# Fewer zero stores inside the groups of an attention-and-FFN backward kernel, the others issued after all compute, and the first weight load issued by ACT

## The chip, the cores and the metric

The kernel runs on one core of one Trainium2 chip. The metric is the device time in microseconds (us) of one execution. A time is the median of several executions. Every comparison was made in rounds on one chip (each of the three sets of experiments on a chip of its own), and runs marked slow (over 1.5% above the fastest of the same kernel) are left out of the ratios.

## The reference

A decode step of a parallel block is differentiated. In short form, the forward pass and what is returned are

```python
xn  = layernorm(x)                                       # x: 4 x 1 x 512, bf16
out = x + attention(xn; k_cache, v_cache, wq, wo) + (gelu(xn @ w_gate) * (xn @ w_up)) @ w_down
# attention: 32 query heads, 8 KV heads, Dh = 128; caches of 4096 positions, of which
# only the last W = 1024 are used:  k = k_cache[:, :, Sk - W:, :]
_out, _vjp = jax.vjp(f, x, k_cache, v_cache, wq, wo, w_gate, w_up, w_down)
return (_out, *_vjp(grad_out))
```

The outputs are `out` and eight gradients. Those of the two caches (`out_2`, `out_3`: 4 x 8 x 4096 x 128) are exactly zero in their first 3072 positions, since the window never reads them. Writing these zeros is 50.3 MB of the 112.4 MB that the kernel moves. They depend on nothing, so the kernel may write them at any time.

## The kernel before

The engines are named as in the profile. In this kernel PE does matmuls and transposes, DVE, ACT and POOL the elementwise work and copies, and SP, ACT and POOL issue transfers (DMA). The tiles that PE writes lie in PSUM here (names in `_ps`); copying a result out of one is called an evacuation. "Granted clock" is the profile's figure for the share of PE's full clock that it was given.

The kernel works through a feed-forward part and then four groups of two KV heads each. (Code below is cut to the lines that matter; `...` marks what is left out.) A zero store is one transfer of 3.146 MB from a tile of zeros, issued by ACT. There are sixteen (`zlist`). A small edge of order ties each to the last evacuation that ACT has been given so far.

```python
    ZG = 4
    zlist = [(og, b, g) for b in range(B) for g in range(0, G, ZG) for og in (out_2, out_3)]

    def zeros(n):
        zsrc = bass.AP(tensor=ztile.tensor, offset=ztile.offset, ap=[list(ztile[:].ap[0]), [0, ZG], [1, ZW]])
        for _ in range(min(n, len(zlist))):
            og, b, g = zlist.pop(0)
            z = store(nc.scalar, og[b, g:g + ZG, 0:K0, :].rearrange("g (m j) d -> m g (j d)", m=P), zsrc, "zeros",
                      ["rest", "zeros"])
            if last_act:
                tc.add_manual_dep(z.ins, last_act[-1].ins.name, ...NoSync...)
```

In the two score passes of a group, each block of K (then of V) is transposed on PE, copied from PSUM by DVE, and multiplied. A queue of small pieces of other work (`tick`) fills in. Each pass issues two zero stores:

```python
    def scores(t, k):
        # ... lf = masked queries (k = 0) or output gradients (k = 1)
        for g in range(GP):
            for b in range(B):
                T_ps = ps_w.tile([P, J, P], BF16, name="T_ps", tag="w")
                for j in range(J):
                    nc.tensor.transpose(T_ps[:, j, :], blks[(t, g)][:, b, j, :], ident[:])
                T_sb = tsb.tile([P, J * P], BF16, name="T_sb", tag="T", bufs=4)
                evac(T_sb[:], T_ps[:].rearrange("p j m -> p (j m)"), 1024, half=True)
                for q in range(NQ):
                    nc.tensor.matmul(ps[q * RG:(q + 1) * RG, :], lhsT=..., rhs=T_sb[...], ...)
                tick(2)
                if b == 1:
                    zeros(1)
```

The feed-forward part issues one more (`zeros(1 if og is out_6 else 0)`). All loads are on SP, in program order. The compiler's scheduler decides the order of the other engines' instructions; only SP is kept in program order.

```python
        nc.sync.dma_start(out=wg_sb[:], in_=B_w_gate...)     # then wu_sb, wd_sb, and the first groups' data
        # ...
        for t in range(NT):
            pre(t); masks(t)
            scores(t, 0); softmax(t);   dvdk(t, 0)
            scores(t, 1); softmax_d(t); dvdk(t, 1)
            odq(t, 0); odq(t, 1)        # od matmuls: values with P, keys with dS
            fin(t); load_next(t); dw(t)
        tick(len(bg))
        # ... two small outputs, issued by ACT
```

## Time and profile before

| | kernel before |
|---|---|
| median | 301.78 us (4 runs, 297.4 to 303.23; the two above 303 count as slow) |
| span of the profiled run | 297.0 us |
| busy shares | PE 71%, DVE 49%, ACT 38%, POOL 22% |
| moved | 112.38 MB, 378 GB/s over the span |
| mean granted clock of PE | 0.838 |

The strip of the page cuts the span into 40 slices; a digit is the busy share of a slice in tenths. The strip, the waits and the group starts stand in the prediction below. The short reading is that the transfers are full almost everywhere (the DMA row is 9 in 35 of 40 slices) and PE is not (71% busy).

### The profile page before, as it was taken

What the parts mean: (1) busy time and instruction counts of PE and PEld (TensorE: products, weight loads), DVE (VectorE), ACT (ScalarE), POOL (GpSimd) and SP (SyncE); (2) the same over time, 40 slices, a digit from 0 to 9 for tenths busy, and PEclk for the clock granted to TensorE, in tenths of its full rate; (3) what the DMA queues carried; (4) which work ended last, traced back from release to release, by engine and by line L of the source; (5) the groups of instructions that cost most, each with busy time, mean ns of one, the idle gap of its engine ahead of it and who ended that gap; (6) DMA issues with size and microseconds to landing.
All of it is one profiled execution on the core that took longest, in us unless ns stands there. A gap on an engine that the chain in (4) does not pass through costs nothing.

```text
span 297.0 us, 6830 instructions
## 1 busy us (share of the span) xinstructions
PE 209.5 (71%) x2956; PEld 144.7 (49%) x2956; DVE 144.7 (49%) x309; ACT 114.0 (38%) x217; POOL 66.4 (22%) x84
## 2 busy tenths in 40 slices
PE   1249897963977997587799066986941976869941
PEld 0249575741645774364576033754731544546321
DVE  6236574433553575345367023453640553544956
ACT  3010464543440665334166023442440453524850
POOL 6000112340303143310314302303010523130230
PEclk9999999695796899779699757697795697986995
DMA  5999999999999999999999999999999799993693
GB/s 150 401 350 386 395 418 397 408 419 424 421 415 414 384 370 419 416 420 418 418 418 421 416 421 420 419 414 418 417 413 404 280 389 391 389 400 146 239 340 131
DMA packets 34149, 112.38 MB, mean 378 GB/s; under 512 B 1408, under 2 KB 7560, under 8 KB 34120
## 3 DMA queue, kind: packets, MB, share of 16 engines
q10 hardware_dynamic: 8464, 50.34, 41.3%
q1 hardware_dynamic: 17848, 30.93, 28.3%
q0 software_dynamic: 7808, 30.67, 26.2%
q8 instruction: 23, 0.38, 0.5%
q14 instruction: 6, 0.05, 0.0%
HBM read 30.93 MB, written 81.01 MB: 377 GB/s over the span
## 4 chain that ended last, share of the span: by engine, by line
DMA 43%; PE 36%; DVE 11%; ACT 3%; issue 3%; POOL 1%; SPq 1%; DVEq 0%; ACTq 0%; POOLq 0%
DMA kb<-in_A_k_cache_dram 26%; PE T_ps L316 8%; DMA out_dram<-osb_o 6%; DMA wd_sb<-in_B_w_down_dram 6%; DVE T_sb L94 5%; PE kv_ps L424 5%; PE S_ps L321 3%; DMA out_dram<-osb_d 3%; DMA out_dram<-osb_g 3%; PE od_ps L396 2%; PE wdT_ps L561 2%; PE wqT_ps L488 2%; PE dwo_ps L443 2%; PE acc_ps L168 1%; PE dwg_ps L607 1%
## 5 line engine op out<-in xcount | busy, mean ns | idle before, releaser
L94 DVE COPY T_sb<-T_ps 128x1024 bf16<-128x1024 bf16 x64 | 44.2, 691 | 47.5 <-PE T_ps L316 47.3
L92 ACT CAST stg_dv<-kv_ps 128x512 bf16<-128x512 f32 x52 | 28.4, 588 | 30.7 <-PE kv_ps L424 30.4
L316 PE MATMUL T_ps<-ident,kb 128*128 128x128 bf16 x256 | 26.1, 245 | 19.0 <-DMA kb<-in_A_k_cache_dram 19.0
L316 PEld LDWEIGHTS <-kb 128*128 128x128 bf16 x256 | 19.9, 111 | 28.5 <-DMA kb<-in_A_k_cache_dram 19.6
L92 ACT CAST stg_dk<-kv_ps 128x512 bf16<-128x512 f32 x46 | 25.2, 588 | 12.8 <-PE kv_ps L424 12.1
L316 PE MATMUL T_ps<-ident,vb 128*128 128x128 bf16 x256 | 25.7, 247 | 0.3 <-DVE osb_q L94 0.3
L424 PE MATMUL kv_ps<-domr,P_q 128*128 128x512 bf16 x64 | 23.5, 441 | 0.0
L316 PEld LDWEIGHTS <-vb 128*128 128x128 bf16 x256 | 19.6, 112 | 6.0 <-issue 1.8
L92 ACT CAST osb_o<-dwo_ps 128x512 bf16<-128x512 f32 x23 | 12.9, 588 | 21.5 <-PE dwo_ps L443 21.0
L92 ACT CAST osb_g<-dwg_ps 128x384 bf16<-128x384 f32 (+1 forms) x30 | 14.7, 532 | 16.6 <-PE dwg_ps L607 8.7
L424 PE MATMUL kv_ps<-qmr,dS_q 128*128 128x512 bf16 x64 | 20.7, 394 | 0.5 <-ACT stg_dv L92 0.2
L92 ACT CAST osb_q<-dwq_ps 128x512 bf16<-128x512 f32 x25 | 13.7, 588 | 16.9 <-PE dwq_ps L458 10.4
L98 POOL DMA_DIRECT2D out_dram<-stg_dv x8 | 6.2, 776 | 40.3 <-ACT stg_dv L92 25.3
L94 DVE COPY wqT<-wqT_ps 128x1024 bf16<-128x1024 bf16 x16 | 11.0, 690 | 8.2 <-PE wqT_ps L488 8.1
L321 PE MATMUL S_ps<-T_sb,qm 128*32 128x256 bf16 x128 | 9.9, 302 | 6.9 <-DVE T_sb L94 6.8
L94 DVE COPY woT<-woT_ps 128x1024 bf16<-128x1024 bf16 x16 | 11.1, 692 | 6.3 <-PE woT_ps L268 6.3
L488 PEld LDWEIGHTS <-wq_sb 128*128 128x128 bf16 x128 | 11.4, 124 | 5.5 <-issue 4.9
L458 PE MATMUL dwq_ps<-od_r,xnm 128*128 128x256 bf16 x64 | 12.9, 328 | 1.2 <-DVE osb_q L94 1.0
L92 ACT CAST osb_d<-dwd_ps 128x512 bf16<-128x512 f32 x14 | 8.0, 590 | 14.5 <-PE dwd_ps L595 14.3
L321 PE MATMUL S_ps<-T_sb,dom 128*32 128x256 bf16 x128 | 10.0, 298 | 5.0 <-DVE T_sb L94 5.0
L321 PEld LDWEIGHTS <-qm 128*32 128x32 bf16 x128 | 4.7, 94 | 17.6 <-issue 15.8
L488 PE MATMUL wqT_ps<-ident,wq_sb 128*128 128x128 bf16 x128 | 13.3, 267 | 0.0
(186 smaller groups left out, 376.8 us busy)
## 6 DMA issues: line engine op xcount, KB each, us to landing
out_dram<-ztile ACTq DMA_DIRECT2D x16, 3072.0 KB, 18.5
kb<-in_A_k_cache_dram SPq DMA_DIRECT2D x8, 1024.0 KB, 12.1
vb<-in_A_v_cache_dram SPq DMA_DIRECT2D x8, 1024.0 KB, 24.6
out_dram<-stg_dv POOLq DMA_DIRECT2D x8, 1024.0 KB, 10.5
out_dram<-stg_dk POOLq DMA_DIRECT2D x8, 1024.0 KB, 11.0
wo_sb<-in_A_wo_dram SPq DMA_DIRECT2D x4, 1024.0 KB, 26.7
wq_sb<-in_A_wq_dram SPq DMA_DIRECT2D x4, 1024.0 KB, 30.5
out_dram<-osb_o POOLq DMA_DIRECT2D x8, 512.0 KB, 9.5
```

Of the source, the lines that this page charges most:

```text
L92: last_act.append(nc.scalar.copy(out=out, in_=in_))
L94: return nc.vector.tensor_copy(out=out, in_=in_)
L98: d = eng.dma_start(out=out, in_=in_)
L168: nc.tensor.matmul(ps[:, c, :], lhsT=lf(c), rhs=rhs, start=(k == 0), stop=(k == len(terms) - 1))
L316: nc.tensor.transpose(T_ps[:, j, :], blks[(t, g)][:, b, j, :], ident[:])
L321: nc.tensor.matmul(ps[q * RG:(q + 1) * RG, :], lhsT=lf[:, s * RG:(s + 1) * RG], rhs=T_sb[:, q * WQ:(q + 1) * WQ], start=(g == 0 and b == 0 ...
L396: nc.tensor.matmul(od_ps[b * RB:b * RB + rep, k, g, :], lhsT=pT[:, jj, c0:c0 + rep], rhs=blks[(t, g)][:, b, j, :], start=(j == 0), stop=(j ...
L424: nc.tensor.matmul(mps[:].rearrange("p b d -> p (b d)"), lhsT=src[:, q, jj * P:(jj + 1) * P], rhs=mr[:, g].rearrange("p b d -> p (b d)"), ...
L443: nc.tensor.matmul(mps[:], lhsT=o_r[:, g, :], rhs=dym[:, i, :], start=True, stop=True)
L458: nc.tensor.matmul(mps[:, i].rearrange("p g d -> p (g d)"), lhsT=xnm[:, i2 * 2 + i, c * P:(c + 1) * P], rhs=dq_r[:].rearrange("p g d -> p ...
L488: nc.tensor.transpose(wT_ps[:, i, c, :], wq_sb[:, c, h * Dh:(h + 1) * Dh], ident[:])
L561: nc.tensor.transpose(wT_ps[:, i, c, :], wd_sb[:, 2 * f2 + i, c * P:(c + 1) * P], ident[:])
```

## The change

The intent is to free the compute from the competition of the zero stores: one in each group, the others when nothing else is left to be disturbed. The load of the first weight moves to ACT, so that it starts beside SP's two small loads. The two small outputs move to SP, away from the long queue on ACT.

```diff
-                if b == 1:
+                if b == 1 and g == 1 and k == 0:
                     zeros(1)
@@
-        nc.sync.dma_start(out=wg_sb[:], in_=B_w_gate.rearrange("(c p) f -> p c f", p=P))
+        nc.scalar.dma_start(out=wg_sb[:], in_=B_w_gate.rearrange("(c p) f -> p c f", p=P))
@@
         tick(len(bg))
+        zeros(len(zlist))
@@
-        nc.scalar.dma_start(out=out_0..., in_=out_b[0:P:RB, :])
+        nc.sync.dma_start(out=out_0..., in_=out_b[0:P:RB, :])
@@
-        nc.scalar.dma_start(out=out_1..., in_=dx_b[0:P:RB, :])
+        nc.sync.dma_start(out=out_1..., in_=dx_b[0:P:RB, :])
```

More of the change, by code (lines that the diff above doesn't have):

```diff
@@ L676 @@
         nc.vector.tensor_tensor(out=out_b[:], in0=acc_o, in1=x_b[:], op=ALU.add)
-        nc.scalar.dma_start(out=out_0.rearrange("b s d -> (b s) d"), in_=out_b[0:P:RB, :])
+        nc.sync.dma_start(out=out_0.rearrange("b s d -> (b s) d"), in_=out_b[0:P:RB, :])
         s1 = tail.tile([P, 1], FP32, name="s1")
@@ L694 @@
         nc.vector.tensor_tensor(out=dx_b[:], in0=pr[:], in1=dy_b[:], op=ALU.add)
-        nc.scalar.dma_start(out=out_1.rearrange("b s d -> (b s) d"), in_=dx_b[0:P:RB, :])
+        nc.sync.dma_start(out=out_1.rearrange("b s d -> (b s) d"), in_=dx_b[0:P:RB, :])
 _INS = ['A_x', 'A_k_cache', 'A_v_cache', 'A_wq', 'A_wo', 'B_x', 'B_w_gate', 'B_w_up', 'B_w_down', 'grad_out']
```

## The prediction

Passages are cut out, with the cuts marked. The sum stands: 259 + 82 + 5 + 2 = 348 us of span, plus 1.7, about 350, put down as 349. The 82 us follow from the trace: 34.6 MB take 82.8 us at the 418 GB/s of many full slices and 81.6 at the 424 of the best one. The 2 us for the last landing are an estimate that fits the kernel before, where the issue of the last store ended at 294.98 us and the span at 297.0. That fewer stalls would make matmuls faster was the estimate from the one stretch quoted, where PE's clock was 0.56 after 9 us without work.

> **What bounds the kernel now.** I read the page first: the strip of 40 slices (7.4 us each), then the queues.
>
> ```profile
> PE   1249897963977997587799066986941976869941
> PEclk9999999695796899779699757697795697986995
> DMA  5999999999999999999999999999999799993693
> GB/s 150 401 350 386 395 418 397 408 419 424 421 415 414 384 370 419 416 420 418 418 418 421 416 421 420 419 414 418 417 413 404 280 389 391 389 400 146 239 340 131
> ...
> q10 hardware_dynamic: 8464, 50.34, 41.3%
> q1 hardware_dynamic: 17848, 30.93, 28.3%
> q0 software_dynamic: 7808, 30.67, 26.2%
> ```
>
> The reader is to see that the DMA row is 9 nearly everywhere while PE has holes. The transfers are the bound from slice 2 to slice 31, at 415 to 421 GB/s in most slices. The queue lines say what moves. q10, on which ACT issues, carries only the zero stores (16 of 3,072 KB = 3.146 MB each, 50.34 MB) and two tiny outputs. q1 has the loads (30.93 MB), q0 the computed gradients (30.67 MB). The three shares sum to 95.8%, some 285 us of full DMA work in a span of 297.0 us, so the kernel stands within about 12 us of its own transfers. Most of that loss is at the two ends (slices 1, 32, 37 to 40).
>
> Next the waits of PE, longest first, which say what the transfers cost the compute:
>
> ```profile
> PE T_ps L316 <- DMA kb<-in_A_k_cache_dram: 19.0, 2, 10.1
> PE S_ps L321 <- DVE T_sb L94: 11.8, 26, 0.8
> ...
> PE f_ps L672 <- ACT osb_q L92: 3.7, 1, 3.7
> ...
> PE dwg_ps L607 <- DVE osb_g L94: 3.5, 1, 3.5
> ...
> PE dwg_ps L607 <- ACT osb_g L92: 1.8, 1, 1.8
> ```
>
> Only 19.0 us of PE idleness is put down to late K blocks (8.9 and 10.1 us). Another 3.5, 1.8 and 3.7 us are evacuations that waited for an output buffer still being stored: ACT and DVE show waits for the stores of osb_g and osb_o in their own wait lists. That is 28 us in all that contention with the zero stores could have caused. The rest of PE's waits are short handoffs that stay. The chain of waits names the two K transfers:
>
> ```profile
> 144.15 28.48 DMA kb<-in_A_k_cache_dram
> ...
> 181.67 47.35 DMA kb<-in_A_k_cache_dram
> ```
>
> A 1,024 KB load takes 28 and 47 us to land because zero stores and gradients are ahead of or between it.
>
> Last the pace of the four groups, from the timeline of POOL, where dS_q is made once per group:
>
> ```profile
> 90.75 1.89 POOL L332 TENSOR_TENSOR dS_q<-dS_b,qmsk 128x1024 bf16<-128x1024 bf16 x1 [8.43 <-DVE dS_b L385]
> ...
> 142.20 1.88 POOL L332 TENSOR_TENSOR dS_q<-dS_b,qmsk 128x1024 bf16<-128x1024 bf16 x1 [8.36 <-DVE dS_b L385]
> ...
> 203.81 1.88 POOL L332 TENSOR_TENSOR dS_q<-dS_b,qmsk 128x1024 bf16<-128x1024 bf16 x1 [7.67 <-DVE dS_b L385]
> ...
> 265.22 1.89 POOL L332 TENSOR_TENSOR dS_q<-dS_b,qmsk 128x1024 bf16<-128x1024 bf16 x1 [0.71 <-DVE dS_b L385]
> ```
>
> The column in front is the start in us. The periods are 51.5, 61.6 and 61.4 us. The second and third contain the 8.9 and 10.1 us of waiting for K; without them they are 52.7 and 51.3 us. So a group costs **about 51.8 us of compute** even when its data is there, of which PE is busy 43 to 44 us (42.85 us in the stretch from 204 to 266 us).
>
> [...]The best slice here is 424, so the zero stores alone can't go much faster than now. [...]after the idle stretch from 220 to 229 us the granted clock of 229 to 236 us is 0.56. Fewer stalls may therefore save a few us of slow matmuls beside the stalls themselves.
>
> **The change part by part.**
>
> *Zero stores.* Before, the feed-forward part issues one and each of the two score passes of a group two, until all sixteen are out; their issues run from 30.3 to 252.6 us. After, one goes out in the feed-forward part and one in each of four groups. The remaining eleven come after all compute in program order. I built the changed kernel and listed its order by engine: the eleven stand together behind ACT's very last evacuation (osb_q), with nothing after them, so no scheduler moves them forward. [...]Eleven stores are 11 x 3.146 = 34.6 MB; [...]nothing but the last gradients is left to lie beside them.
>
> *What compute gains.* Everything else to be moved until then is 30.93 + 30.67 + 5 x 3.146 = 77.3 MB, or 185 us at 418 GB/s, less than the compute needs. So the groups become bound by PE and its handoffs. First dS_q: 90.75 less the osb_g waits (5.3) gives 85.5 us. Three more groups of 51.8 us: 241 us. From the last dS_q to the end of ACT's last evacuation there are 289.7 - 265.2 = 24.5 us before, of which 3.5 us was the wait for osb_o's store; that leaves 21 us, so ACT reaches the eleven stores at **about 262 us**, or a few us sooner if the PE clock stays up. I take 258 to 260. The gain of compute is thus some 30 us against 289.7.
>
> *What the end costs.* From 259 us: 82 us of zeros; some 2 MB of gradients issued in the last us share the engines, 5 us; 2 us for the last landing. The span is 259 + 82 + 5 + 2 = 348 us. The time of the profiled run was 298.75 for a span of 297.0 us, so add 1.7: about 350 us; I say **349 us**.
>
> *wg on ACT.* SP issues x_b at 0.81, dy_b at 1.56, wg at 2.16, each taking about half a us. On ACT wg can start some 1.4 us earlier. PE waits 3.2 us for wg at its first product, so up to 1.4 us can be won there; but wd lands at 20.9 us after 5.5 MB of weights, a matter of rate, and wg will now share the engines with x_b, which heads the normalisation. I count 0 to 1 us, inside the range.
>
> *The two small outputs on SP.* There they need not queue behind the eleven stores on ACT; they are ready long before the zeros end, so they cost nothing.
>
> **The rivals.** (a) *Compute, freed of contention, ends so early that the tail fits.* To equal 303 us, ACT would have to finish by 303 - 1.7 - 89 = 212 us. Busy PE alone is 209.5 us, and in the first 10 us PE has only 1.4 us of work. It would take groups of under 40 us, below PE's 43 us of busy time. Only a clock near 1.0 (mean now 0.838) would come near. Two thirds of the way, groups of 45 us, would give about 328 us. (b) *Only the transfers count, and their order is free.* Then the time stays 285 us of work plus the ends, about 297 to 303 us or a little less by quicker starts. Against it: before the tail the engines would have to stay full, and 77.3 MB do not fill 259 us: 74 us of DMA time stand empty. (c) *A single queue of stores alone runs below 418 GB/s.* Nothing in the trace shows zeros alone; at 380 GB/s the tail would be 91 us and the time near 358 us. (d) *Load waits stay in spite of fewer zeros*, because gradients and prefetches still collide when a group ends; the kernel would be up to 10 us slower still.
>
> **Range and chances.** The centre is 349 us. Faster groups pull down by up to 14 us, a slower tail or left waits push up by as much: 335 to 363 us. For a time within 2% of 303 us (below 309) compute would have to run faster than PE's busy time allows, so I give same 0.02, faster 0.01, slower 0.97.
>
> **What the profile after would show.** The strip should show DMA well below 9 in the middle (about 280 to 330 GB/s on average over the groups), then ten to eleven slices near 420 GB/s with PE at 0. The waits of PE for kb should fall from 19 us to under 5; dS_q should come every 50 to 52 us, the last at 236 to 243 us; eleven issues of ztile should stand in one run at 255 to 263 us. The chain should end in a transfer out of ztile of about 80 us. I am wrong if the groups drop to 45 us or less, if the tail runs at a rate far from 418 GB/s, or if the tail's issue comes before compute ends.

## The result

The changed kernel takes 332.56 us (4 runs, 331.54 to 335.36), the kernel before 301.78 us. The ratio is 1.114, with a 95% interval of 1.098 to 1.129: slower by 11%. Ratios here are the mean time of one kernel's fast runs over that of the other's of the same rounds, so they are not quite the ratio of the medians: two of the four runs of the kernel before are slow (303.01 and 303.23), and the mean of its other two is 298.98. The direction was right. The median lies 16 us under the predicted 349 and just below the low end of the range, 335.

The strip of the changed kernel (a slice is now 8.3 us):

```profile
PE   0359897969899588998788995979820000000000
PEclk9998999969999879799799996998965555555555
DMA  7999999794699995999967659831999999999998
GB/s 271 321 361 385 403 407 408 275 409 174 204 383 409 420 407 208 323 389 413 421 253 253 263 200 384 307 131 56 345 374 407 415 413 416 414 410 415 417 418 331
```

The reader is to see three stretches. Up to slice 7 the transfers are as full as before. In slices 8 to 28 the row of GB/s has holes that the zero stores used to fill (174, 204, 208, 131, 56 GB/s), while PE is denser than it was. From slice 31 on PE is 0 and the transfers run near 415 GB/s, with nothing beside them.

The end of ACT's timeline gives the boundary; the columns are start, duration (both us), engine, line, operation:

```profile
241.34 0.59 ACT L92 CAST osb_q<-dwq_ps 128x512 bf16<-128x512 f32 x1 [3.50 <-DMA out_dram<-osb_o]
241.39 1.78 ACTq L98 DMA_DIRECT2D out_dram<-ztile  x2
241.83 0.59 ACT L92 CAST osb_q<-dwq_ps 128x512 bf16<-128x512 f32 x1
243.21 54.00 ACTq L98 DMA_DIRECT2D out_dram<-ztile  x9
```

Of the eleven issues the first took ACT 0.38 us and the last nine 54.0 together, which cost nothing here, as ACT had no more compute. Compute on ACT ends at 242.4 us and the span at 330.2, so the tail is 87.8 us. The prediction had 259 and 89. The missing time is thus in the compute, and POOL's timeline tells where:

```profile
85.07 1.89 POOL L332 TENSOR_TENSOR dS_q<-dS_b,qmsk 128x1024 bf16<-128x1024 bf16 x1 [0.64 <-DVE dS_b L385]
...
130.03 1.89 POOL L332 TENSOR_TENSOR dS_q<-dS_b,qmsk 128x1024 bf16<-128x1024 bf16 x1 [0.97 <-DVE dS_b L385]
...
175.41 1.89 POOL L332 TENSOR_TENSOR dS_q<-dS_b,qmsk 128x1024 bf16<-128x1024 bf16 x1 [0.97 <-DVE dS_b L385]
...
218.91 1.89 POOL L332 TENSOR_TENSOR dS_q<-dS_b,qmsk 128x1024 bf16<-128x1024 bf16 x1 [0.84 <-DVE dS_b L385]
```

The first falls where it was predicted (85.07 against 85.5). The periods are 45.0, 45.4 and 43.5 us, 44.6 on average, against the predicted 51.8. The waits of PE (us in total, times, longest us):

```profile
PE tps L196 <- DMA dy_b<-in_grad_out_dram: 9.5, 1, 9.5
PE f_ps L673 <- ACT osb_q L92: 3.7, 1, 3.7
...
PE pT_ps L341 <- DVE dS_b L385: 3.0, 4, 0.9
...
PE S_ps L321 <- DVE T_sb L94: 2.0, 5, 0.6
```

The 19.0 us for kb are gone, as expected. Two things were not expected. The wait of the scores matmuls for DVE's copy (T_sb) fell from 11.8 us to 2.0, although neither those copies (691 ns before and after) nor any transfer stands between the two. And PE's first transposes wait 9.5 us for dy_b, where it was 3.6.

The copies are no faster, yet PE waits less for them: the order in which PE does its work must have changed. The compiled programs can be listed. Of PE's 5,866 rows the two kernels have between 4,996 and 5,198 in common order, depending on how the listings are matched; a few rows of DVE and POOL stand elsewhere too (9 of 309 and 3 of 87). The last blocks of the first score pass of the second group show the pattern; Tk are transposes of K, S the scores matmuls, dwo pieces of other work, each with its count:

```
before:  S:4  Tk:8  S:4  dwo:2  Tk:8  dwo:2  S:4  Tk:8  dwo:2  Tk:7  S:4 ...
after:   Tk:8  dwo:1  S:4  dwo:1  Tk:4  S:4  Tk:4  dwo:2  Tk:7  S:4  Tk:1  dwo:2  Tk:7  S:4 ...
```

Before, some of the S stand directly behind their own block's transposes and have to wait for the copy. After, four or more of the eight transposes of the next block run first, and the copy is done meanwhile. Why the compiler places them so was not studied. In the second pass there is one more difference: before, 64 od matmuls of the values stand amid the scores of the pass; after, most of them come behind it and fill the time in which PE waits for the softmax (its wait for dS_b fell from 4.9 to 3.0 us).

### The profile page after: what moved, and what is told of

The parts are those of the page before. It is cut to its first block, busy times and chain, and to the rows that moved or that the text cites. A ratio compares the mean times of both kernels' runs of the same rounds, so it can differ in the third digit from the quotient of the medians.

```text
span 330.2 us, 6826 instructions
## 1 busy us (share of the span) xinstructions
PE 194.6 (59%) x2956; PEld 135.4 (41%) x2956; DVE 144.6 (44%) x309; ACT 113.1 (34%) x217; POOL 66.6 (20%) x84
## 4 chain that ended last, share of the span: by engine, by line
PE 44%; DMA 17%; DVE 7%; ACT 4%; issue 3%; SPq 1%; ACTq 0%; DVEq 0%; POOLq 0%
DMA out_dram<-osb_o 9%; PE T_ps L316 9%; PE kv_ps L424 8%; DMA wd_sb<-in_B_w_down_dram 6%; PE S_ps L321 4%; PE wqT_ps L488 3%; PE acc_ps L168 2%; DMA out_dram<-osb_d 2%; PE wgT_ps L634 2%; PE woT_ps L268 2%; PE wdT_ps L561 2%; PE dwg_ps L607 2%; PE od_ps L396 2%; PE dwo_ps L443 1%; ACT stg_dk L92 1%
## 5 line engine op out<-in xcount | busy, mean ns | idle before, releaser
L316 PE MATMUL T_ps<-ident,kb 128*128 128x128 bf16 x256 | 23.3, 220 | 0.2 <-ACT osb_g L92 0.2
L316 PEld LDWEIGHTS <-kb 128*128 128x128 bf16 x256 | 17.4, 97 | 9.8 <-issue 1.8
L424 PE MATMUL kv_ps<-domr,P_q 128*128 128x512 bf16 x64 | 21.2, 404 | 0.0
L424 PE MATMUL kv_ps<-qmr,dS_q 128*128 128x512 bf16 x64 | 19.6, 378 | 0.7 <-ACT stg_dv L92 0.3
L94 DVE CAST stg_dk<-kv_ps 128x512 bf16<-128x512 f32 x18 | 12.1, 686 | 1.4 <-PE kv_ps L424 1.0
L94 DVE COPY wgT<-wgT_ps 128x1024 bf16<-128x1024 bf16 x14 | 9.6, 692 | 6.3 <-PE wgT_ps L634 6.2
L488 PEld LDWEIGHTS <-wq_sb 128*128 128x128 bf16 x128 | 9.7, 110 | 4.6 <-issue 3.2
L488 PE MATMUL wqT_ps<-ident,wq_sb 128*128 128x128 bf16 x128 | 11.4, 242 | 0.1
L268 PE MATMUL woT_ps<-ident,wo_sb 128*128 128x128 bf16 x128 | 11.2, 218 | 0.4 <-ACT stg_dv L92 0.2
L98 POOL DMA_DIRECT2D out_dram<-osb_d x4 | 3.1, 785 | 39.8 <-ACT osb_d L92 39.8
```

The costliest lines, as they stand in the source:

```text
L94: return nc.vector.tensor_copy(out=out, in_=in_)
L98: d = eng.dma_start(out=out, in_=in_)
L268: nc.tensor.transpose(wT_ps[:, i, c, :], wo_sb[:, 2 * h2 + i, c * P:(c + 1) * P], ident[:])
L424: nc.tensor.matmul(mps[:].rearrange("p b d -> p (b d)"), lhsT=src[:, q, jj * P:(jj + 1) * P], rhs=mr[:, g].rearrange("p b d -> p (b d)"), ...
L488: nc.tensor.transpose(wT_ps[:, i, c, :], wq_sb[:, c, h * Dh:(h + 1) * Dh], ident[:])
```

## The experiments

Two theories for the short groups went to the chip. Theory O: the compiler placed PE's instructions in another order, and that is worth the 7 us of a group. Theory C: the zero stores had slowed the compute in ways that the list of waits does not show. Conveniently, some edits move the traffic and leave PE's order exactly as it was. This was checked on the compiled programs: run 1 has the order of the kernel before on PE, DVE, POOL and SP, and runs 2, 3, 5 and 9 have that of the changed kernel.

**1. The order of the kernel before, with little traffic.** All sixteen zero stores keep their places but write 16 of 128 partitions (two outputs wrong). The orders on PE, DVE, POOL and SP are exactly those of the kernel before.

```diff
-  og[b, g:g + ZG, 0:K0, :].rearrange("g (m j) d -> m g (j d)", m=P), zsrc, "zeros",
+  og[b, g:g + ZG, 0:K0, :].rearrange("g (m j) d -> m g (j d)", m=P)[0:16], zsrc[0:16], "zeros",
```

> The kernel before with each of its 16 zero stores cut to 16 of its 128 partitions (0.39 MB in place of 3.15; the zero outputs are wrong on purpose). The order of instructions on PE is exactly that of the kernel before. What is disputed: the groups of the changed kernel take 44 to 45 us, where the prediction had 51.8. Theory O (order): the compiler placed PE's instructions in another order, and that is worth some 6 us a group. Then the groups here stay at 50 to 52 us although nothing contends, the span is some 270 us and the time 272. Theory C (contention): the zero stores slowed compute in ways that the list of waits does not show. Then the groups here fall to 44 to 46 us, the span is some 250 us and the time 252.

It took 273.38 us, with a span of 271.3; dS_q started at 88.69, 140.01, 190.15 and 239.80 us. The periods are 51.3, 50.1 and 49.7 us, as theory O said. The largest wait of PE in this run:

```profile
PE S_ps L321 <- DVE T_sb L94: 12.4, 28, 0.8
PE pT_ps L341 <- DVE dS_b L385: 4.9, 4, 1.2
```

The wait for kb is gone, and the waits that come of the order stay as they were before (11.8 and 4.9 us). The stretch of one group in three kernels, a line each, shows what a group loses. The columns are the stretch, its length, busy us of PE, PEld, DVE, ACT and POOL with their instruction counts, PE clock, DMA share, GB/s. First the kernel before:

```profile
90.75:142.20 51.45, 41.54 (x586) 28.38 (x587) 26.59 (x54) 22.98 (x44) 13.54 (x12) 0.87 1.02 406
```

Then this experiment:

```profile
88.69:140.01 51.32, 40.57 (x586) 27.85 (x587) 26.72 (x54) 22.97 (x44) 13.54 (x13) 0.90 0.90 278
```

And the changed kernel:

```profile
85.07:130.03 44.96, 38.71 (x586) 26.44 (x587) 26.79 (x55) 22.77 (x44) 13.61 (x13) 0.92 0.93 355
```

PE does the same 586 matmuls in all three. Removing a third of the bytes (406 to 278 GB/s; the engines are still busy for 0.90 of the time) saves 0.1 us; the other order saves 6.4. Over the three periods, PE is idle for 9.8 us of each in this experiment and for 6.0 in the changed kernel, and busy for 40.6 against 38.6 us at a clock of 0.89 against 0.92. So two thirds of the gain of some 5.8 us is idleness and one third faster matmuls. PE's wait for T_sb falls from 12.4 us to 2.0 in the whole run, which over the four groups is some 2.6 of the 3.8 us of idleness a group. The size has a margin: runs 5 and 9 below, which are the changed kernel up to the tail, have periods of 45.5 and 45.6 us on average in place of 44.6, so the order is worth some 5 to 6 us.

**2. The order of the changed kernel, two zero stores per group.**

```diff
-                    zeros(1)
+                    zeros(2)
```

> The changed kernel with two zero stores in each group at the same place in place of one, so seven at the end. PE's order is exactly that of the changed kernel. Traffic of a group 12.6 + 6.3 = 18.9 MB, at 418 GB/s 45 us. Theory O: groups 45 to 47 us, compute ends at about 248, tail 7 x 7.5 + 7 = 60 us, span 308, time 310. Theory C: the second store lengthens the groups by about 3 us each, compute ends at about 258, span 318, time 320.

307.13 us (ratio 1.032 to the kernel before; 1.022 to 1.041). Periods of 45.3, 49.1 and 45.9 us, 46.7 on average; the tail starts at 250.0. Theory O had said groups of 45 to 47 us, 248 and 310 us, theory C groups some 3 us longer than the changed kernel's, 258 and 320. The end of compute and the time lie near theory O. The groups are 2.1 us longer than the changed kernel's and 1.2 longer than those of runs 5 and 9, so doubling the zero stores is not quite free, but the pace stays well below the 50.4 us of the order before.

**3. The same with three per group** (`zeros(3)`).

> As the run before with three per group, so three at the end. A group moves 22.0 MB, 53 us at 418 GB/s, so the groups are bound by transfers in either theory: 53 us each, compute ends at about 270, tail 3 x 7.5 + 7 = 30 us, span 293 to 300. Theory O says 293 to 297, time 296, a little faster than the kernel before, as PE catches up whenever data are there. Theory C says as the kernel before, 300 to 303. If ACT is held at the third issue of a burst, as it is at the end of the changed kernel, a group may be longer by that.

297.01 us, ratio 0.997 (0.988 to 1.005): the same as the kernel before. The time fits the 296 of theory O, but the kernel before ran faster in these rounds too (its fast runs took 295.7 to 299.9), and "as the kernel before" is what theory C had said. This run does not separate the two. The groups take 49.4, 53.6 and 54.8 us and are bound by transfers again (395, 411 and 377 GB/s, DMA share 1.03, 1.03 and 0.95); PE waits 16.9 us for kb. So nothing is won over the kernel before, but the loss of the changed kernel is gone, by moving only stores. As for the hold of ACT that the expectation names: at the end of the changed kernel the first four issues of zero stores took 0.38, 1.36, 1.36 and 6.75 us, so the long hold came with the fourth.

**4. The load of wg on SP again**, in the changed kernel.

```diff
-        nc.scalar.dma_start(out=wg_sb[:], ...)
+        nc.sync.dma_start(out=wg_sb[:], ...)
```

> The changed kernel with the load of wg issued by SP again. In the changed kernel x_b and dy_b land later beside wg: PE's first transposes start at 12.3 us in place of 6.4, and wd's first transposes at 21.9 in place of 21.0. Theory 1: the load on ACT costs about 1 to 2.5 us; time 330 to 331.5. Theory 2: the first weights are bound by the rate, nothing changes: 332.5. PE's order differs in 148 of 5,866 rows, so up to 2 us either way may come from that.

331.75 us; ratios to the kernel before of 1.115 (this) and 1.114 (the changed kernel), which do not differ beyond noise. The traces show where the two differ. PE's first transposes start at 6.40 us here and at 12.32 in the changed kernel, where wg is issued at 0.81 us, with x_b (0.81) and before dy_b (1.60); here it is issued behind both. The transposes of wd start at 20.74 against 21.93 us, the first dS_q at 84.17 against 85.07.

```profile
6.40 0.61 PE L196 MATMUL tps<-ident,dy_b 128*128 128x128 bf16 x4 [3.55 <-DMA dy_b<-in_grad_out_dram]
```

```profile
12.32 0.61 PE L196 MATMUL tps<-ident,dy_b 128*128 128x128 bf16 x4 [9.48 <-DMA dy_b<-in_grad_out_dram]
```

The first line is this run, the second the changed kernel. The load on ACT thus costs some 1.2 us at the transposes of wd, not the 6 us of the small loads. PE waits for wd in both (0.9 us here, 3.6 in the changed kernel), and wd is the last of three weights of 1.8 MB each. From 10 to 22 us, while wu and wd land, the transfers run at 372 GB/s in the kernel before and 345 in the changed kernel. That delay is seen in all six traces compared: 20.74 to 21.00 us with the load on SP (this run, the kernel before, run 1), 21.93 to 22.26 with it on ACT (the changed kernel, runs 2 and 3). At the first dS_q the size is not known: runs 5 and 9, the same program as the changed kernel up to there, have it at 87.88 and 87.05. As 148 rows of PE's order differ too, I do not claim the last tenths.

**5. The tail with stores of 16 partitions** in the changed kernel (two outputs wrong): `[0:16]` as in experiment 1, for the eleven last stores alone.

> The changed kernel with each of the eleven last stores cut to 16 of 128 partitions (two zero outputs wrong on purpose), PE's order exactly that of the changed kernel. If the tail is a matter of bytes, 34.6 MB become 4.3: the groups stay at 44 to 45 us, the last dS_q at 219, compute ends at 242, and the span is 242 plus some 12 to 16 us: 254 to 258, time 256 to 260, so that 74 to 78 us of the changed kernel's 332 are the tail's. If the tail cost time for another reason (ACT held by its issues, a slow queue), the span stays over 280.

A miss: 295.11 us with a span of 294.4, where 254 to 258 was expected. The groups kept 45.1 to 46.0 us, but the tail ran at a quarter of the rate:

```profile
260.00:270.00 10.00, 0.00 (x0) 0.00 (x0) 0.00 (x0) 0.00 (x0) 0.00 (x0) 0.50 0.97 102
```

The columns are as above: 102 GB/s with the DMA engines busy for 97% of the time. My edit was at fault: it cut partitions and bytes together. From 260 to 290 us its stores of 16 partitions moved 101 to 102 GB/s, where the stores of all 128 moved 412 to 418 in the changed kernel's tail (250 to 328 us). What holds the narrow stores back is not shown by any run here. This run says nothing against bytes as the cause of the tail. The stores of experiment 1 have the same 16 partitions, and there too the engines were busier than the bytes suggest (DMA share 0.90 at 278 GB/s, beside 0.93 at 355 in the changed kernel), which makes that comparison of orders fairer.

**6. The order of the kernel before without the hoisted od matmuls**, traffic as in experiment 1 (two outputs wrong). One edge of order is added:

```diff
+        st[t]["last_mm"] = mm                       # the last scores matmul of the pass
@@ odq: each od matmul
+                    tc.add_manual_dep(mm.ins, st[t]["last_mm"].ins.name, ...NoSync...)
```

> The first experiment (order of the kernel before, zero stores at an eighth) with one edge of order added: the matmuls of od for the values may not start before the last scores matmul of the second pass. This takes one of the two differences of order away; the other, that the transposes of the next block are queued ahead of the scores matmul of this one, stays as in the kernel before. If the hoisted od matmuls make the long groups, the periods fall from 50-51 us to 45-46 and the span to about 256. If the blocks' order does, PE still waits some 12 us in all for T_sb and the periods stay at 49 to 51, the span at 268 to 272. A share each: 47 to 48 us.

265.47 us, span 264.3; periods 48.3, 51.4 and 47.0, 48.9 on average against 50.4 in experiment 1. The hoisted od matmuls are a smaller share, some 1.5 us a group. PE's wait for T_sb rose to 15.5 us: the other difference remains.

**7 and 8. Three stores per group with wg on SP**, a second store in the feed-forward part, and two at the end. Number 7 has two stores in the first pass and one in the second; number 8 spreads them, one in each pass and one after the second softmax.

```diff
# 7
-                if b == 1 and g == 1 and k == 0:
-                    zeros(1)
+                if b == 1 and g == 1:
+                    zeros(2 - k)
@@
-                    zeros(1 if og is out_6 else 0)
+                    zeros(1)
# 8: zeros(1) at the same condition, and after softmax_d(t):
+            zeros(1)
```

> A candidate to beat both: wg on SP as before; two zero stores in the feed-forward part, and in each group two in the first score pass and one in the second, at places that leave PE's order in the score passes that of the changed kernel; two stores at the end. Transfers are to be full all the time: 112.4 MB at some 400 GB/s are 281 us, with some 5 us at each end about 288 to 294. Theory O: 291, 2 to 4% faster than the kernel before. If late loads hold PE as in the kernel before (19 us), 296 to 300, no gain.

> As the run before, with the three of a group spread: one in the first score pass, one in the second, one after the second softmax. Each burst is shorter, so loads should land earlier: PE's wait for kb under 10 us in place of 17 to 19, time 288 to 293. If bursts do not matter, the same as the run before within 1%.

Number 7 took 296.19 us, ratio 0.985 (0.977 to 0.992). The 291 us of theory O were missed: late loads held PE, as its other branch (296 to 300) had it. Number 8 took 299.37 us with two of its four runs slow, ratio 0.988 (0.975 to 1.000), so it does not differ from number 7 for certain. Its expected 288 to 293 us was missed. Its one profile (wait for kb of 19.3 us) is of a slow run, so it is not compared. In number 7, PE's timeline shows one long stop:

```profile
215.56 0.71 PE L316 MATMUL T_ps<-ident,kb 128*128 128x128 bf16 x5 [14.08 <-DMA kb<-in_A_k_cache_dram]
```

The K block was issued at 166.53 us, just before a pair of zero stores (167.3), and landed 49 us later. While PE stood, nothing new was produced to store, and in the 6 us from 220 us on the engines moved 12 GB/s. The late load cost twice here: 14.1 us of PE, then 6 us of nearly empty engines.

**9. A quarter of the tail over all partitions**, to mend experiment 5. Each of the eleven last stores writes one head of four (0.79 MB; two outputs wrong).

```diff
+    def zeros(n, zg=ZG):
-  og[b, g:g + ZG, 0:K0, :]..., zsrc, ...
+  og[b, g:g + zg, 0:K0, :]..., zsrc[:, 0:zg], ...
-        zeros(len(zlist))
+        zeros(len(zlist), 1)
```

> The run with the little tail again, as its stores of 16 partitions ran at 101 GB/s and so told little. Now each of the eleven last stores reads all 128 partitions and writes one head of four, 0.79 MB in place of 3.15 (two zero outputs wrong on purpose); PE's order exactly that of the changed kernel. If the tail is bytes at the full rate, 8.65 MB take some 21 us where 34.6 MB took some 83: compute ends at 242 to 247, the span is 268 to 274, time 270 to 276. If something else holds the tail, the span stays over 290.

272.43 us, span 272.4. The tail begins at 246.3 and lasts 26.1 us; in the changed kernel it began at 241.4 and lasted 88.8. So 62.7 us went with 26.0 MB (11 x 0.75 x 3.146), which is 414 GB/s. (Counted from the last dS_q to the end of the span, 111.3 us there and 48.6 here, it is 62.7 too.) At that rate the 8.65 MB that are left take 20.9 of the 26.1 us; the other 5 us I put down, as an estimate, to the last gradients and the landing. The zero stores' part of the tail is thus bytes at that rate. The groups were 45.4, 45.4 and 45.9 us, once more.

**10. Both differences of order taken away from the kernel before**, traffic as in experiment 1 (two outputs wrong): the edge of experiment 6, and the transposes of the next block emitted ahead of this block's scores matmul.

```diff
+        nxt = tr(*order[0])                          # transposes and copy of a block
         for g in range(GP):
             for b in range(B):
-                T_ps = ...; transposes; T_sb = ...; evac(...)
+                T_sb = nxt
+                i = g * B + b
+                if i + 1 < len(order):
+                    nxt = tr(*order[i + 1])
```

> The first experiment (kernel before, zero stores at an eighth) with both differences of order taken away as far as program order allows: transposes of the next block are emitted ahead of this block's scores matmul, and the od matmuls of the values come after the last scores matmul. With the od edge alone the periods were 48.3, 51.4 and 47.0 us and PE waited 15.5 us in all for T_sb. If the blocks' order is the rest, the wait for T_sb falls under 6 us and the periods to 44.5 to 46.5, the span to 250 to 257, time 252 to 259. If not, they stay at 48 to 51 and some third thing of the order is at work.

262.12 us, span 258.7; periods 47.2, 50.9 and 44.9, on average 47.7. The scores matmuls' wait for T_sb is gone from the list; other PE lines now carry waits for T_sb of 2.9, 1.9, 0.8, 0.6 and 0.2 us, 6.4 together, just over the expected 6. But the periods come down only half of the way, from 50.4 to 47.7 with 44.6 to be reached (45.5 in runs 5 and 9), and the span misses its range (250 to 257 us) by 2 us and the time (252 to 259) by 3. The order here is not that of the changed kernel either (over 500 of PE's rows still stand elsewhere), and this run does not say which of the other differences make up the rest.

**11 and 12. Fewer zero stores where K was starved.** Number 11 is number 7 with only one store in the first pass of the third group, so three at the end. Number 12 adds the transposes-ahead edit of experiment 10.

```diff
-                    zeros(2 - k)
+                    zeros((2 - k) if t != 2 else 1)
```

> The candidate with two in the first pass and one in the second, but one and one in the third group, where PE waited 14.1 us for kb behind them; three stores at the end. If the zeros of the third group starve kb, that wait falls under 6 us, compute ends some 6 us sooner, and with one store of 7.5 us more in the tail the time is 294 to 297, as the candidate's 296.2 within 1%. If transfers that were idle for 8 us at 219 to 226 us fill too, 289 to 293.

> As the run before, with the transposes of the next block emitted ahead of this block's scores matmul. Where transfers bound the groups this changes nothing (same within 1% of the run before); where PE does, it takes away its waits for T_sb and compute ends 2 to 5 us sooner, so up to 1.5% less time.

Number 11 took 290.69 us, ratio 0.974 (0.964 to 0.983): the fastest correct kernel, beating both. Of the seven runs of the kernel before in these rounds, four were slow and are left out; the three fast ones took 298.1 to 298.8 us. Number 12 took 291.46 us, ratio 0.977 (0.974 to 0.980), no different: in this kernel, which is full of transfers, the other order of PE bought nothing. The strip of number 11 and its longest wait of PE for a load:

```profile
DMA  4999999999999999999999999999999999999997
GB/s 143 401 352 381 399 415 415 412 402 394 415 418 400 372 353 402 413 418 418 417 416 419 411 398 419 411 423 412 410 362 396 396 396 401 357 351 383 413 417 312
```

```profile
PE T_ps L316 <- DMA kb<-in_A_k_cache_dram: 5.7, 2, 4.6
```

The DMA row is now 9 from slice 2 to slice 39. Three zero stores lie behind the compute and fill the hole that the kernel before had at its end (146, 239, 340 and 131 GB/s in slices 37 to 40; here 383, 413, 417 and 312), and PE's longest stop for K is 4.6 us in place of 14.1 in number 7. The measured time lies in the better of the two ranges expected (289 to 293).

## Why the prediction was right or wrong

**The direction and its reason were right.** The prediction said that the kernel is bound by its transfers and that the changed kernel leaves the engines part empty and then runs alone through 34.6 MB. The strip shows both, and experiment 9 shows that the tail is bytes at 414 GB/s. That the groups would be bound by PE and its handoffs was right as well; how long these take was not.

**The tail was right**: 89 us predicted from the start of the eleven stores, 88.8 measured.

**The first group was right in sum, with luck**: 85.5 against 85.07 us, and 87.05 and 87.88 in runs 9 and 5 of the same program. The waits for osb_g that were subtracted (5.3 us) fell to 2.4 and not to 0, and the order differs in this group too. The part for wg had the wrong sign: 0 to 1 us of gain was allowed, and experiment 4 shows some 1.2 us of cost at the transposes of wd. The prediction named wg's load beside x_b as a cost, but not its weight.

**The step that failed is the pace of the groups**: "So a group costs **about 51.8 us of compute** even when its data is there". It was measured at 44.6, and the prediction's own sign of being wrong, groups of 45 us or less, came true. Three periods make 21.6 us of the miss against the sum of 262 us. The prediction had already taken some 3 us of that for a better clock (259), and the wait for osb_o before the last evacuations stayed (3.5 us), so that the stretch from the last dS_q to the end of ACT's compute was 23.5 us and not 21. That wait had been read as contention with the zero stores, which it was not. The store of osb_o takes as long in the kernel before (first line) as in the changed kernel, at 340 and 342 GB/s, and the zero store before it had been issued 31 and 40 us earlier, where none took more than 28.7 and 33.4 us to land (columns: start, duration in us):

```profile
284.01 4.50 DMA out_dram<-osb_o
```

```profile
236.74 4.51 DMA out_dram<-osb_o
```

The figure of 51.8 us itself was well read: experiment 1 shows that the kernel before, freed of seven eighths of its zero bytes, has periods of 50.4 us, so the waits that I subtracted were nearly all that this traffic cost, and theory C is left with 1.4 us a group. The order has some 5 to 6. What failed is the silent premise that the changed kernel's PE would do its work in the same order. I had built it and listed the order, but used only the end of ACT's. That PE's listing differed in hundreds of rows, I passed over. Experiments 2, 5 and 9 have exactly the changed order and show 45 to 46 us in eight of nine groups (49.1 once), with single or double zero traffic and with different tails.

**A rival had it nearly right.** "Two thirds of the way, groups of 45 us, would give about 328 us" stood under rival (a), and was passed over because matching the old time would take groups under 40 us. Its floor did not hold either: PE's 43 to 44 us of busy time a group (41.5 to 44.1 in the periods of the trace) fell to 38.6.

**What stays open.** Exact pairs of orders show that the order is worth some 5 to 6 us a group. Its two visible differences account for part of it: some 1.5 us for the od matmuls and some 1.2 us more for the blocks ahead (experiments 6 and 10). The other 2 to 3 us lie in differences that were not tried one by one. A part goes with the granted clock, 0.92 in the changed kernel's groups and 0.89 in experiment 1's, but the clock also differs between executions of one program (0.872 to 0.888 over the four of experiment 1). No run here separates the gaps from the clock.

## What to carry to other kernels

If a kernel is near the bound of its transfers, as this one was (285 us of DMA work in a span of 297.0), a store that depends on nothing is filling: give it to the stretches where the engines would be empty, the end included, and keep it away from the load that compute needs next (number 11: ratio 0.974). Moving eleven of the sixteen to the end only turned hidden bytes into visible time here: the tail took 87.8 us, at 412 to 418 GB/s, and the ratio was 1.114. And where a compiler orders the instructions, compare the order on every engine before you carry a pace from the old trace to the new kernel: moving a few stores and one load reordered a tenth or more of PE's instructions here (some 670 to 870 of 5,866 rows), and the order alone was worth some 5 to 6 us of every group of 50.
